# A gated linear attention with a maxout FFN: the carried state as a dense tile, its products with q per head, and a new order of all steps

## The chip, the cores and the metric

The kernel runs on one core of a Trainium2 chip. The metric is the device time of one execution in microseconds (us). All times here are of the same inputs, drawn once.

## The reference, cut to what matters

```python
# q, k, v, alpha: 4 x 8 x 768 x 48 (batch, heads, sequence, head size)
for t in range(S):
    state = alpha[:, :, t, :, None] * state + einsum('bhd,bhe->bhde', k[:, :, t], v[:, :, t])
    y[:, :, t] = einsum('bhd,bhde->bhe', q[:, :, t], state)
x = y.transpose(0, 2, 1, 3).reshape(3072, 384)
h = maximum(maximum(x @ w1, x @ w2), x @ w3)      # 384 -> 768
out = h @ w_out                                   # 768 -> 384
```

The first part is a recurrence over 768 positions with a state of 48 x 48 numbers for each of 32 heads; the second an ordinary matrix product with a maximum of three.

## The kernel before

**Tiling of the attention.** Each of the 12 windows `n` covers 256 positions of one batch (`c = n // 4` is the place in the sequence, `b = n % 4` the batch), all 8 heads. A position pair lies on one of 128 partitions (index `r` is which of the pair). The 128 partitions hold two sub-blocks `i` of 64 pairs, that is of 128 positions each. A window is worked in two units `u = 2n, 2n + 1` of four heads, counted in the texts as the even and the odd unit. Heads come in couples: `j` is the couple, `p` the head in it, and head `p` of a couple lies on partitions 64p to 64p + 47 once transposed.

**Steps of the attention.** `decay` squares alpha's pairs (`aa`), takes logarithms (`la`), and computes the factors by which the state decays (`hp`, `e`, `G`). `prep` sums the logarithms with a matmul (`Lp`, line 426), takes exponentials and scales q and k by them (`qk`, line 440) and v (`v`), then transposes q and k (`tp`, line 465) and evicts them (`qkT`, line 479). `attend` computes the scores of a unit as 16 small matmuls (`A`, line 491), and DVE masks and evicts them as `LA` (line 499). `state` sums k v over a sub-block (`pp`, line 523), and carries the state on: `grown` adds the decayed state to the sum (`add`, line 412, into `U` or `V`), `carry` decays it (`Z`, line 400). `output` multiplies q by the carried state (`yi`, line 556) and the scores by v (`ya`, line 578), both into the same PSUM bank, one bank for each sub-block; `xb` scales the result into SBUF, `xp` turns it (line 599), and `xT` holds the FFN's input.

**How the carried state is kept.** For each sub-block `i` and batch `b` there is a tile `Zs[i][b]` of 128 rows by 4 couples by 96 columns in 16 bits. Head 0 of a couple stands on rows 0 to 47 and columns 0 to 47, head 1 on rows 64 to 111 and columns 48 to 95; all else is zero from a memset at the start (line 228). So one matmul with 128 rows and 96 columns gives both heads' product with q. `carry` and `grown` write and read the two corners with an instruction each, on 48 rows.

**The FFN.** It is max(x w1, x w2, x w3) = x w1 + max(0, x (w2 - w1), x (w3 - w1)). `differences` makes the two differences (`d`, line 308) once the weights are there. `ffn` computes for each window 6 gate steps (`gp`, line 622, 6 matmuls of 256 columns each); ACT or DVE takes the positive part of the first of each couple (`h0`, lines 631 and 633), DVE the maximum with the second (`h1`, line 638). `op` then multiplies x by `past` = w1 w_out (line 655) and h by w_out (line 658) into one bank; `ob` evicts it and `out` stores it. `past` itself is computed once by `bypass` (`wt`, `w1T`, `mp`, line 334).

**The order.** Nothing is scheduled at run time. Each call of `plan.step` adds a step with its dependences, and `emit` walks through the string `ORDER`, one token for each step: its number, the letter of the engine that gets it (P for PE, V for DVE, A for ACT, G for POOL, S for SP), and the PSUM banks. Each engine then works its own steps strictly in that order. Loads and outputs are issued on SP, the four weight loads (`w1s`, two halves of `wcat`, `wo`) on POOL, between its other steps. There are 8 PSUM banks, shared by all.

## Time and profile before

| | us |
|---|---|
| median of 3 runs | 151.62 |
| lowest and highest | 150.16, 151.63 |
| the profiled execution, first to last instruction (its span) | 148.5 |
| lies around the span, by the lowest and the median run | 1.6 to 3.1 |
| PE busy | 130.6 (88% of the span) |
| DVE busy | 121.9 (82%) |
| ACT busy | 80.7 (54%) |
| POOL busy | 71.8 (48%) |

The profile is of an execution of its own, whose time outside the span isn't recorded; it is bounded by the runs. Busy time of PE is from modelled ends, and two small matmuls in different parts of the array count as one stretch. In the lists a row gives line, engine, operation, what it writes and reads, the shape, the count, then busy time and the mean in nanoseconds of one, then the idle time ahead of it and what ended that. PEld is the loading of the stationary operand.

### The profile page before, as it was taken

The numbers are of one execution on the slowest core, as the hardware profiler recorded it, in microseconds if no ns is written. First come the engines' busy times: TensorE is split into PE (matmuls) and PEld (weight loads), VectorE is DVE, ScalarE is ACT, GpSimd is POOL, SyncE is SP. The second block draws the span as 40 slices with busy tenths as digits, with TensorE's granted clock in tenths as the row PEclk, the third lists the DMA queues.
The fourth block names the chain that finished last, engine by engine and source line by source line (L and its number), as shares of the span: only waits on it lengthen the run. The fifth ranks groups of instructions, "written<-read, shape, count | busy, mean of one in ns | idle before, by whom it ended". The sixth has DMA issues, their size and how long they took to land.

```text
span 148.5 us, 5617 instructions
## 1 busy us (share of the span) xinstructions
PE 130.6 (88%) x2389; PEld 101.7 (68%) x2389; DVE 121.9 (82%) x231; ACT 80.7 (54%) x182; POOL 71.8 (48%) x114
## 2 busy tenths in 40 slices
PE   0136588889999999999999999999999999999990
PEld 0025576767776678887687889777777788787670
DVE  6489996999899979998896899699698786789720
ACT  3665156796895987947877759328622820000011
POOL 8105810431859888999976678994720100000000
PEclk9999999999999999999999999999999999999999
DMA  4999999999999999999997299601211100031223
GB/s 111 257 261 262 258 214 212 279 231 265 270 262 265 261 275 267 262 288 268 233 279 188 79 246 280 200 3 60 106 57 57 53 4 0 4 119 40 85 99 134
DMA packets 54728, 26.34 MB, mean 177 GB/s; under 512 B 50736, under 2 KB 54320, under 8 KB 54704
## 3 DMA queue, kind: packets, MB, share of 16 engines
q1 hardware_dynamic: 53584, 23.60, 63.4%
q0 software_dynamic: 832, 2.36, 8.1%
q8 instruction: 18, 0.29, 0.9%
q10 hardware_dynamic: 288, 0.04, 0.3%
q14 instruction: 6, 0.05, 0.1%
HBM read 23.63 MB, written 4.72 MB: 191 GB/s over the span
## 4 chain that ended last, share of the span: by engine, by line
PE 65%; DMA 10%; POOL 6%; ACT 5%; DVE 4%; SPq 4%; issue 3%; POOLq 0%; DVEq 0%
PE psum L622 26%; PE psum L658 15%; PE psum L655 8%; DMA wcat<-in_moe_w_dram 6%; SPq L274 4%; DMA qn<-in_q_dram 4%; POOL qk L440 3%; PE psum L491 3%; PE psum L578 3%; PE psum L465 2%; PE psum L599 2%; PE psum L334 2%; PE psum L556 2%; PE psum L523 2%; POOL Z L400 1%
## 5 line engine op out<-in xcount | busy, mean ns | idle before, releaser
L622 PE MATMUL psum<-xT,d 128*128 128x256 f16 x432 | 54.1, 273 | 0.9 <-DVE d L308 0.5
L622 PEld LDWEIGHTS <-d 128*128 128x128 f16 x432 | 40.0, 98 | 7.0 <-DVE d L308 1.5
L499 DVE TENSOR_TENSOR LA<-psum,d 128x1024 f16<-128x1024 f32 x24 | 28.7, 1218 | 3.7 <-PE psum L491 2.8
L658 PE MATMUL psum<-wo,hT 128*128 128x384 f16 (+1 forms) x150 | 27.5, 320 | 0.0
L638 DVE TENSOR_TENSOR hT<-psum,hT 128x512 f16<-128x512 f32 x36 | 23.7, 681 | 2.9 <-PE psum L622 2.6
L440 POOL TENSOR_TENSOR qk<-qn,ep 128x384 f16<-128x384 f32 x18 | 18.3, 1026 | 11.3 <-DMA qn<-in_q_dram 9.2
L631 ACT ACTIVATE hT<-psum 128x512 f16<-128x512 f32 x28 | 16.4, 601 | 12.7 <-PE psum L622 12.3
L255 ACT COPY ob<-psum 128x384 f32<-128x384 f32 x14 | 6.7, 481 | 27.8 <-PE psum L658 27.8
L658 PEld LDWEIGHTS <-hT 128*128 128x128 f16 x150 | 14.5, 98 | 8.9
L440 POOL TENSOR_TENSOR qk<-kn,en 128x384 f16<-128x384 f32 x16 | 15.9, 999 | 9.0 <-ACT en L435 8.5
L479 DVE COPY qkT<-psum 128x1024 f16<-128x1024 f16 x24 | 16.0, 683 | 0.9 <-PE psum L465 0.7
L655 PE MATMUL psum<-past,xT 128*128 128x384 f16 (+1 forms) x75 | 15.8, 320 | 0.0
L259 ACT ACTIVATE xb<-psum,c 128x384 f16<-128x384 f32 x17 | 9.3, 583 | 9.0 <-PE psum L578 9.0
L435 ACT ACTIVATE en<-psum 128x384 f32<-128x384 f32 x24 | 11.5, 493 | 2.1 <-DVE psum L430 2.1
L465 PE MATMUL psum<-d,qk 64*128 64x64 f16 x384 | 8.8, 198 | 4.1 <-POOL qk L440 2.1
L435 ACT ACTIVATE ep<-psum 128x384 f32<-128x384 f32 x24 | 11.6, 493 | 1.1 <-DVE psum L430 0.8
L351 POOL TENSOR_TENSOR aa<-an 128x384 f32<-128x384 f32 x9 | 9.0, 1001 | 4.7 <-DVE qkT L479 4.2
L255 ACT CAST xT<-psum 128x384 f16<-128x384 f32 x20 | 9.4, 482 | 3.0 <-PE psum L599 2.8
L426 PE MATMUL psum<-la,c 128*128 128x192 f16 x24 | 6.1, 271 | 5.5 <-ACT la L361 5.5
L465 PEld LDWEIGHTS <-qk 64*128 64x128 f16 x384 | 7.0, 99 | 5.5 <-DVE qk L440 2.9
L400 POOL TENSOR_TENSOR Z<-U,G 48x192 f16<-48x192 f32 x10 | 5.0, 504 | 11.8 <-DVE U L412 11.5
L430 DVE TENSOR_TENSOR psum<-psum,la 128x192 f32<-128x192 f32 x24 | 8.5, 358 | 2.6 <-PE psum L426 1.8
(58 smaller groups left out, 196.4 us busy)
## 6 DMA issues: line engine op xcount, KB each, us to landing
out_dram<-ob SPq DMA_DIRECT2D x23, 192.0 KB, 2.0
an<-in_alpha_dram SPq DMA_DIRECT2D x11, 384.0 KB, 6.2
qn<-in_q_dram SPq DMA_DIRECT2D x11, 384.0 KB, 5.7
kn<-in_k_dram SPq DMA_DIRECT2D x11, 384.0 KB, 6.2
vn<-in_v_dram SPq DMA_DIRECT2D x11, 384.0 KB, 6.3
wcat<-in_moe_w_dram POOLq DMA_DIRECT2D x2, 576.0 KB, 10.3
w1s<-in_moe_w_dram POOLq DMA_DIRECT2D x1, 576.0 KB, 7.9
wo<-in_moe_w_out_dram POOLq DMA_DIRECT2D x1, 576.0 KB, 7.8
```

Source lines behind the costliest of these rows:

```text
L255: (nc.scalar.copy if eng == "ACT" else nc.vector.tensor_copy)(out=out, in_=in_)
L259: nc.scalar.activation(out=out, in_=in_, func=AFT.Copy, scale=factor)
L435: lambda eng, t=t, sign=sign: nc.scalar.activation(out=t, in_=live[Lk], func=AFT.Exp, scale=sign),
L440: lambda eng, w=w, x=x, e=e: on[eng].tensor_mul(qk[:, w, :, :, :D].rearrange("p r h d -> p h r d"), ld[x][n % NL][:, hs], e),
L465: nc.tensor.transpose(live["tp", v][:, i, at:at + HALF], qks[v % NQ][rows, w, r, 2 * j:2 * j + 2, :], ident[rows, rows])
L479: lambda eng: nc.vector.tensor_copy(out=qkT.rearrange("p i w j t -> p i (w j t)"), in_=live["tp", u]),
L499: lambda eng: nc.vector.tensor_mul(LA.rearrange("p a j r t -> p (a j) (r t)"), live[Ak].rearrange("p a (j t) -> p (a j) t", j=2), maskA.un ...
L622: nc.tensor.matmul(live[gk][:, jj, :], hidden(apart[g][j][:, kt], jj), xT[:, kt, :], start=(kt == 0), stop=(kt == NFT - 1))
L631: nc.scalar.activation(out=h, in_=live[gk], func=AFT.Relu)
L638: lambda eng, h=h, gk=gk: nc.vector.tensor_max(h, live[gk], h),
L655: nc.tensor.matmul(live[ok], xT[:, kt, i * P:(i + 1) * P], past[:, kt, cols], start=(kt == 0), stop=False)
L658: nc.tensor.matmul(live[ok], hT[:, kt, i * P:(i + 1) * P], wo16[:, kt, cols], start=False, stop=(kt == NJ - 1))
```

## The change

`Zs` is now 128 rows by 4 couples by 48 columns: each head's state stands on its own rows, and the columns are shared, so the tile is dense (its padding rows hold what the sums give there). `carry` and `grown` are one instruction each over all 128 rows; the memsets of `Zs` are gone.

The product with q is taken per head: 48 rows of q and of the state, 48 columns, 8 matmuls for each sub-block in place of 4. They are split in two halves. The crossed ones, (sub-block 0, head 1) and (sub-block 1, head 0), are a step `yi` of their own for both sub-blocks together; the scores `A` of the odd unit wait for it. The others, (0, 0) and (1, 1), stand within `ya`, which now runs the odd unit's products with v first, then these, then the even unit's. `ya` therefore holds the two banks from `yi` on.

There are 777 steps where there were 821, and `ORDER` is new throughout: places, engines and banks of all steps. Read off the two strings: POOL has 36 `qk`, 16 `v`, 12 `aa` and 8 `Z` (34, 14, 9 and 23 before), DVE 12 `qk`, 1 `aa`, 12 `Z` of both kinds and 16 `add` (14, 4, 17 and 32), 12 `ob`, 9 `h0`, 2 `w1T` and 1 `past` (11, 8, 0 and 0). Ahead of the first gate step PE has the same attention steps of windows 0 and 1. Twelve gate steps of windows 0 and 1 then follow almost in a row, where the order before has ten among the attention of window 2. After the last attention output 12 gate steps are left (15 before). PE's last step is the second part of a half-wide `op` of the last 128 rows (a full-wide `op` before). The load of `w_out` is issued by POOL behind `aa` and `G0` of window 2.

```diff
@@ ORDER: the first and the last line of each @@
-0S 3S 53S 6S 7S 5S 2S 1S 11V 12A 8V 13A 4S 10A 28P0 9A 54S 14P1 29V 17P2 57V 55S 30A 18V 31A 56S
...
-818P 794P7 811A 816S 812S 819V 820S 795A 796S
+3S 11G 0S 1S 8G 9A 13A 26P0 10A 17P7 51S 56A 18V 19A 21G 55V 20A 12A 57A 61P7 27V 29A 71P1 72V 2S
...
+763P6 765P4 769P3 764V 770P 771V 772S 766P 767A 768S 773P6 774P 775A 776S
@@ -194,7 +191,7 @@
     obs = homes(4, [P, DM], FP32, "ob")
     U0s = homes(2, [P, NP, D], FP32, "U")
     U1s = homes(B, [P, NP, D], FP32, "V")
-    Zs = [homes(B, [P, NP, 2 * D], FP16, f"Z{i}_") for i in range(2)]
+    Zs = [homes(B, [P, NP, D], FP16, f"Z{i}_") for i in range(2)]
     e12s = homes(6, [P, NP, UB, 2], FP32, "e")
     G0s = homes(2, [P, NP], FP32, "G")
     G1s = homes(2, [P, NP], FP32, "H")
@@ -223,9 +220,6 @@
         nc.vector.memset(t[:, :, :, D:], 0.0)
     for t in qks:
         nc.vector.memset(t[:, :, :, :, D:], 0.0)
-    for eng, zz in ((nc.gpsimd, Zs[0]), (nc.vector, Zs[1])):
-        for t in zz:
-            eng.memset(t, 0.0)
 
     plan = Plan()
     place = {}
@@ -392,26 +386,17 @@
 
 
     def carry(engines, Zn, U, G, rank, reads, writes):
-        for p in range(2):
-            rows, cols = slice(p * DP, p * DP + D), slice(p * D, (p + 1) * D)
-
-            def run(eng, rows=rows, cols=cols):
-                src = live[U] if isinstance(U, tuple) else U
-                on[eng].tensor_mul(Zn[rows, :, cols], src[rows],
-                                   G[rows].unsqueeze(2).broadcast_to([D, NP, D]))
-
-            plan.step("Z" if "POOL" in engines else "Zp", engines, rank, run,
-                      reads=[U if isinstance(U, tuple) else (*reads[0], p), *reads[1:]],
-                      writes=[(*writes[0], p)])
+        def run(eng):
+            src = live[U] if isinstance(U, tuple) else U
+            on[eng].tensor_mul(Zn, src, G.unsqueeze(2).broadcast_to([P, NP, D]))
+
+        plan.step("Z" if "POOL" in engines else "Zp", engines, rank, run, reads=reads,
+                  writes=writes)
 
 
     def grown(U, key, Z, rank, Zk, to):
-        for p in range(2):
-            rows, cols = slice(p * DP, p * DP + D), slice(p * D, (p + 1) * D)
-            plan.step("add", "DVE", rank,
-                      lambda eng, rows=rows, cols=cols: nc.vector.tensor_add(
-                          U[rows], live[key][rows], Z[rows, :, cols]),
-                      reads=[key, Zk[p]], writes=[(*to, p)], size=0.6)
+        plan.step("add", "DVE", rank, lambda eng: nc.vector.tensor_add(U, live[key], Z),
+                  reads=[key, Zk], writes=[to], size=0.6)
 
 
     def prep(u):
@@ -470,15 +455,16 @@
                   reads=[("qk", v % NQ, w) for v in units for w in range(2)],
                   writes=[tk], size=len(units))
         for v in units:
-            attend(v, tk)
-
-
-    def attend(u, tk):
+            qkT = qkTs[v % NT_]
+            plan.step("qkT", "DVE", v,
+                      lambda eng, v=v, qkT=qkT: nc.vector.tensor_copy(
+                          out=qkT.rearrange("p i w j t -> p i (w j t)"), in_=live["tp", v]),
+                      reads=[tk], writes=[("qkT", v % NT_)])
+
+
+    def attend(u):
+        n, hh = divmod(u, 2)
         qkT, LA, Ak = qkTs[u % NT_], LAs[u % NT_], ("A", u)
-        plan.step("qkT", "DVE", u,
-                  lambda eng: nc.vector.tensor_copy(
-                      out=qkT.rearrange("p i w j t -> p i (w j t)"), in_=live["tp", u]),
-                  reads=[tk], writes=[("qkT", u % NT_)])
 
         def scores(eng):
             live[Ak] = banks2(Ak, FP32)
@@ -494,7 +480,7 @@
                                 qkT[rows, i, 0, j, :], start=True, stop=True)
 
         plan.step("A", "PE", u, scores, banks=[Ak],
-                  reads=[("qkT", u % NT_)], writes=[Ak])
+                  reads=[("qkT", u % NT_)] + [("crossed", n)] * hh, writes=[Ak])
         plan.step("LA", "DVE", u,
                   lambda eng: nc.vector.tensor_mul(
                       LA.rearrange("p a j r t -> p (a j) (r t)"),
@@ -527,7 +513,7 @@
 
         plan.step("pp", "PE", rank, sums, banks=keys, writes=keys,
                   reads=[("qk", u % NQ, 1) for u in us] + [("v16", u % NQ) for u in us])
-        Z0, Z1 = ([("Z", i, b, p) for p in range(2)] for i in range(2))
+        Z0, Z1 = ("Z", 0, b), ("Z", 1, b)
         if c == 0:
             carry("DVE", Zs[1][b], keys[0], G0s[n % 2], rank,
                   [keys[0], ("G0", n % 2)], [("Z", 1, b)])
@@ -540,34 +526,46 @@
             grown(U1s[b], keys[1], Zs[1][b], rank, Z1, ("V", b))
 
 
-    def output(n):
+    def carried(n):
         c, b = divmod(n, B)
         us = (2 * n, 2 * n + 1)
         keys = [("yp", n, i) for i in range(UB)]
         old = [c > 0 or i > 0 for i in range(UB)]
         rank = 2 * n + 1
 
-        def inter(i):
-            live[keys[i]] = bank(keys[i], [P, H, D], FP32)
+        def inter(pairs, first):
             for hh in range(2):
                 qkT = qkTs[us[hh] % NT_]
                 for j in range(2):
-                    h = 4 * hh + 2 * j
-                    nc.tensor.matmul(live[keys[i]][:, h:h + 2, :], qkT[:, i, 0, j, :],
-                                     Zs[i][b][:, 2 * hh + j, :], start=(h == 0), stop=False,
-                                     skip_group_check=True)
-
-        for i in range(UB):
-            if old[i]:
-                plan.step("yi", "PE", rank, lambda eng, i=i: inter(i), banks=[keys[i]],
-                          writes=[keys[i]],
-                          reads=[("Z", i, b, p) for p in range(2)]
-                          + [("qkT", u % NT_) for u in us])
+                    for i, p in pairs:
+                        if not old[i]:
+                            continue
+                        rows = slice(p * DP, p * DP + D)
+                        nc.tensor.matmul(live[keys[i]][:, 4 * hh + 2 * j + p, :],
+                                         qkT[rows, i, 0, j, :], Zs[i][b][rows, 2 * hh + j, :],
+                                         start=(first and hh == 0 and j == 0), stop=False,
+                                         skip_group_check=True)
+
+        def crossed(eng):
+            for i in range(UB):
+                if old[i]:
+                    live[keys[i]] = bank(keys[i], [P, H, D], FP32)
+            inter(((0, 1), (1, 0)), True)
+
+        plan.step("yi", "PE", rank, crossed, banks=[keys[i] for i in range(UB) if old[i]],
+                  writes=[keys[i] for i in range(UB) if old[i]] + [("crossed", n)],
+                  reads=[("Z", i, b) for i in range(UB) if old[i]] + [("qkT", u % NT_) for u in us])
+
+        return inter, keys, old, us, rank
+
+
+    def output(n, inter, keys, old, us, rank):
+        c, b = divmod(n, B)
 
         def intra(hh):
             LA, v16 = LAs[us[hh] % NT_], v16s[us[hh] % NQ]
             for i in range(UB):
-                if hh == 0 and not old[i]:
+                if hh and not old[i]:
                     live[keys[i]] = bank(keys[i], [P, H, D], FP32)
             for j in range(2):
                 for p in range(2):
@@ -577,13 +575,18 @@
                             h = 4 * hh + 2 * j + p
                             nc.tensor.matmul(live[keys[i]][:, h, :], LA[rows, p, j, r, :],
                                              v16[rows, 2 * j + p, r, :],
-                                             start=(h == 0 and r == 0 and not old[i]),
+                                             start=(h == HH and r == 0 and not old[i]),
                                              stop=(r == 1), skip_group_check=True)
 
-        plan.step("ya", "PE", rank, lambda eng: [intra(hh) for hh in range(2)],
+        def attended(eng):
+            intra(1)
+            inter(((0, 0), (1, 1)), False)
+            intra(0)
+
+        plan.step("ya", "PE", rank, attended,
                   banks=[keys[i] for i in range(UB) if not old[i]], writes=keys,
-                  reads=[("LA", u % NT_) for u in us]
-                  + [("v16", u % NQ) for u in us])
+                  reads=[("LA", u % NT_) for u in us] + [("v16", u % NQ) for u in us]
+                  + [("Z", i, b) for i in range(UB) if old[i]] + [("qkT", u % NT_) for u in us])
         for i in range(UB):
             m = 2 * n + i
             xb, yk, xk = xbs[m % 3], keys[i], ("xp", n, i)
@@ -689,7 +692,10 @@
                 for g in WAFTER.get(j, ()):
                     weights(g)
         state(n)
-        output(n)
+        shared = carried(n)
+        for u in (2 * n, 2 * n + 1):
+            attend(u)
+        output(n, *shared)
         if n == 3:
             differences()
             bypass()
```

81 lines of the change are left out of this document (39 added, 42 removed).

## The prediction

> **What bounds the kernel now.** I read the page's busy rows and slices first, then stretches cut at the times where the work changes, then the chain that ended last for the price of each step.
>
> ```profile
> PE 130.6 (88%) x2389; PEld 101.7 (68%) x2389; DVE 121.9 (82%) x231; ACT 80.7 (54%) x182; POOL 71.8 (48%) x114
> PE   0136588889999999999999999999999999999990
> DVE  6489996999899979998896899699698786789720
> PEclk9999999999999999999999999999999999999999
> ```
>
> ```profile
> 0.00:26.00 26.00, 13.00 (x306) 10.07 (x306) 20.62 (x48) 12.93 (x30) 9.69 (x24) 1.00 1.06 225
> 26.00:50.40 24.40, 23.07 (x431) 17.32 (x433) 23.00 (x46) 19.51 (x45) 13.86 (x19) 1.00 1.17 262
> 50.40:101.10 50.70, 50.42 (x1075) 40.66 (x1068) 44.79 (x84) 36.15 (x85) 42.90 (x65) 1.00 0.86 218
> 101.10:145.30 44.20, 44.08 (x593) 33.67 (x592) 33.46 (x57) 11.72 (x26) 5.33 (x9) 1.00 0.17 60
> ```
>
> The four stretches give PE, PEld, DVE, ACT and POOL busy time. Until 26 us PE is half idle and the DMA engines are full (share 1.06). From 26 to 101 PE is nearly always busy, and so is DVE: 23.0 of 24.4, then 44.8 of 50.7. After 101 it is PE alone, at a full clock. A busy PE is not a PE at its peak, though, so I price its steps where they run undisturbed:
>
> ```profile
> 89.90 0.51 PE psum L578 x32
> 90.40 0.47 PE psum L465 x32
> 94.09 0.57 PE psum L491 x32
> 94.66 0.24 PE psum L523 x16
> 98.45 0.49 PE psum L655 x3
> 98.94 0.97 PE psum L658 x6
> 99.91 0.17 PE psum L556 x4
> 100.66 0.40 PE psum L578 x32
> 130.49 4.58 PE psum L622 x42
> 145.22 0.48 ACT ob L255
> ```
>
> ```profile
> 5.49 0.32 PE L426 MATMUL psum<-la,c 128*128 128x192 f16 x1 [5.49 <-ACT la L361]
> ```
>
> The first fence is the chain (start, length, step), the second the timeline of PE, its first matmul. A gate product costs 109 ns (4.58/42), a step of six 0.66 us; a down projection 1.46 us; a small tile 12.5 to 18 ns; a carried product (L556) 42 ns. Times the counts (432, 207 full and 18 half-wide, 384 each of L465, L491 and L578, 320 of L523, 80 of L556, and some 11 us for the rest) this makes about 119 us. PE works from 5.49 to 145.2, 139.7 us, so some 21 us are lost. The 306 matmuls ahead of 26 us (64 in each of the four small-tile steps, 3.8 us, and 50 others, some 2.6) need about 6.4 of 20.5 us: 14 us are lost there, to loads and the first attention chain, and about 7 behind it. So in the middle and end time is PE work, with a small loss that DVE shares in; the end is 3.3 us of eviction and output behind the last matmul.
>
> **Part 1, the carried state.** Today each carry and each sum is two instructions on 48 rows; the change makes it one on 128.
>
> ```profile
> L430 DVE TENSOR_TENSOR psum<-psum,la 128x192 f32<-128x192 f32 x24 | 8.5, 358 | 2.6 <-PE psum L426 1.8
> L412 DVE TENSOR_TENSOR U<-psum,Z 48x192 f32<-48x192 f32 x16 | 5.7, 354 | 2.2 <-PE psum L523 1.9
> L412 DVE TENSOR_TENSOR V<-psum,Z 48x192 f32<-48x192 f32 x16 | 5.5, 351 | 0.3
> L400 POOL TENSOR_TENSOR Z<-V,H 48x192 f16<-48x192 f32 x13 | 6.8, 528 | 1.1 <-DVE H L388 0.6
> L400 POOL TENSOR_TENSOR Z<-U,G 48x192 f16<-48x192 f32 x10 | 5.0, 504 | 11.8 <-DVE U L412 11.5
> L440 POOL TENSOR_TENSOR qk<-qn,ep 128x384 f16<-128x384 f32 x18 | 18.3, 1026 | 11.3 <-DMA qn<-in_q_dram 9.2 <-ACT ep L435 2.0
> L261 DVE TENSOR_SCALAR xb<-psum,c 128x384 f16<-128x384 f32 x7 | 4.3, 611 | 0.2
> ```
>
> DVE takes 0.358 us for 128 rows of 192 (L430) and 0.354 for 48 (L412): rows are free, so the merged instruction keeps the price of one half. Sums: 32 to 16, 16 x 0.353 = 5.6 us less DVE. Carries: 40 to 20; read off the two orders, POOL's go from 23 to 8 (15 x 0.515 = 7.7 us less), DVE's from 17 to 12 (5 x 0.36 = 1.8 less). The memsets of Z go; they run before the first load lands, and are worth nothing. The new order also moves other work: DVE loses three squarings of alpha and two q/k products and gains two w1T copies and single evictions, which about cancel. POOL gains three squarings, two q/k and two v products, which eat most of what it saves (a q/k product is 1.03 there). Net: DVE about 7 us less, POOL and ACT 2 to 5 less.
>
> What is that worth? In 50.4 to 101.1 lie 6.98 us of L412 and 1.74 of DVE's L400:
>
> ```profile
> 50.40:101.10 50.70, 6.98 (x20) 1.00 0.86 218
> 50.40:101.10 50.70, 1.74 (x5) 9.20 (x19) 1.00 0.86 218
> ```
>
> Half, 4.4 us, leaves DVE there. It lies beside PE work; PE at the prices above would need about 48 of those 50.7 us. So the gain is between 0 (cover complete) and 2.7 (all of PE's loss was DVE's). I take 1.0, nearer the low end, since PE's busy row is 50.42 of 50.70. **-1.0.**
>
> **Part 2, the products.** 80 matmuls of 128 rows by 96 become 160 of 48 rows by 48, on the same kind of 64x128 tile as L578's. Those are the nearest row: 12.5 to 16 ns each, since neighbours lie in different halves of the array. 160 x 14 = 2.2 us against 80 x 42 = 3.4: **-1.1**. The change alternates halves too, but only where both sub-blocks have an old state; in the first four windows the four crossed ones all lie in one half. Bounds: at 12.5 ns -1.4; at the old 42 ns each, +3.3.
>
> The Trainium skill ("TensorE: Matmul & The Clock Gate", Back-to-back issue gap and the floors before it) says starts never come closer than about 25 ns however few columns. By that floor the products would cost 160 x 25 = 4.0 us, +0.6 where the sum has -1.1. The trace disagrees for alternating halves: 32 starts in 0.40 us.
>
> **Part 3, the head.** The order of the first eleven loads changes but they are the same ones. DVE now has k of window 1 (qk of unit 2) in front of qkT of unit 1.
>
> ```profile
> 8.10 1.42 SPq L274 DMA_DIRECT2D kn<-in_k_dram  x1
> ```
>
> ```profile
> 26.79 0.82 POOL L288 DMA_DIRECT2D wo<-in_moe_w_out_dram  x1
> ```
>
> ```profile
> 26.04 0.83 PE L622 MATMUL psum<-xT,d 128*128 128x256 f16 x6 [0.51 <-DVE d L308]
> ```
>
> ```profile
> kn<-in_k_dram SPq DMA_DIRECT2D x11, 384.0 KB, 6.2
> wo<-in_moe_w_out_dram POOLq DMA_DIRECT2D x1, 576.0 KB, 7.8
> ```
>
> ```profile
> L499 DVE TENSOR_TENSOR LA<-psum,d 128x1024 f16<-128x1024 f32 x24 | 28.7, 1218 | 3.7 <-PE psum L491 2.8 <-issue 0.7
> L638 DVE TENSOR_TENSOR hT<-psum,hT 128x512 f16<-128x512 f32 x36 | 23.7, 681 | 2.9 <-PE psum L622 2.6
> L479 DVE COPY qkT<-psum 128x1024 f16<-128x1024 f16 x24 | 16.0, 683 | 0.9 <-PE psum L465 0.7
> L308 DVE TENSOR_TENSOR d<-wcat,w1s 128x768 f16<-128x768 f16 x6 | 3.6, 618 | 1.2 <-DMA wcat<-in_moe_w_dram 1.2
> ```
>
> These are the issue of window 1's k on SP, of wo on POOL, PE's first gate product, the times from issue to landing, and DVE's groups. That k lands at about 8.1 + 6.2 = 14.3. Behind it on DVE stand the q/k product, three qkT (0.68), three LA (1.22), four carry steps (0.35), three xb (0.61) and one difference (0.62): about 10 us, so 24.3, and some 1 us of waits between engines. Transposing and one d make the first gate product start at 26 to 26.7 against 26.04, so the memsets and the earlier first weights buy nothing: **+0.3** (0 to 0.7).
>
> From there to 50 us the new order runs twelve gate steps almost in a row: 7.9 us of PE, while DVE has six differences (3.7), two w1T copies (1.2 by the d row) and six h1 (4.1), 9.0 us. DVE is 1 us late there, and wo, which POOL issues only behind G0 of window 2 (and that waits for ACT's e), goes out about 0.8 us later than 26.79 and lands 7.8 after that, just where the product w1 x w_out needs it. The old order loses about 3 us in the same stretch to the same causes. SP's queue holds the same 52 loads and 25 outputs, 36 loads ahead of the first output where it was 32; it gives and costs nothing. I take **0**, from -1.5 (the run is dense) to +2 (both lags land on the chain).
>
> **Part 4, the new wait.** Scores of the odd unit now wait for the crossed products, those for the second state, that for DVE's sum, that for L523. Unhurried: 0.35 + 0.36 to 0.5 + three hand-overs, about 1.2 us. The order sets other PE work between: in window 4 a score step, two gate steps and a turn, 0.28 + 0.66 + 0.66 + 0.17 = 1.8 us; in window 6 2.7. Queued behind the crossed step on PE are the scores, then gate steps, and behind these the evictions. With that cover: 0. The attended step now takes the odd unit's LA first, which is ready last; that removes 0.2 us of cover, which other steps replace.
>
> **Part 5, the tail.** The last PE step is now a half-wide one. Its eviction falls from 0.48 to about 0.3 and its output from 192 to 96 KB:
>
> ```profile
> out_dram<-ob SPq DMA_DIRECT2D x23, 192.0 KB, 2.0
> out_dram<-ob SPq DMA_DIRECT2D x2, 96.0 KB, 1.7
> L255 DVE COPY ob<-psum 128x192 f32<-128x192 f32 x2 | 0.7, 358 | 2.0 <-PE psum L658 1.9
> ```
>
> 0.2 + 0.3, less a little since two other outputs go out just before it: **-0.4** (-0.6 to +0.3).
>
> **Sum.** -1.0 - 1.1 + 0.3 + 0 + 0 - 0.4 = -2.2 on a span of 148.5, 146.3. The runs have 151.62 as median and 150.16 as lowest, so 1.6 to 3.1 us lie around the span; that stays. Predicted 149.4; its own range, from the bounds above, is 148.2 to 150.4.
>
> **Rivals.** (a) DVE's relief counts in full: 2.7 instead of 1.0, and the dense run at 26 us brings its 1.5, so 146.2 to 147.7, about 147.0. For it: DVE's 23.0 of 24.4. Against: PE's 50.42 of 50.70. Chance 0.15. (b) It is hidden: DVE's time lies beside PE's and only products and tail count, less the head and a little of DVE's lag (+0.6): -1.1 - 0.4 + 0.3 + 0.6 = -0.6, 151.0. The 25 ns case lands here too. Chance 0.22. (c) Slower: the crossed products arrive late. If DVE stands in an LA (1.22) when L523 ends, and POOL in a q/k product (1.0) when the sum is done, the chain is 1.22 + 0.35 + 1.0 + 0.5 + 0.3 = 3.4 against 1.8 to 2.7 of cover: about 1 us lost in each of windows 4 to 9, and PE in order stands still for it. -2.2 + 6 = +3.8: 155.4. For it: POOL is 42.9 of 50.7 busy in 50 to 101, and its Z today waits 11.5 us for U without harm only because nothing in front of the scores needs it. Against: in most windows the order puts sum and carry of the state on DVE directly ahead of LA. It decides once the windows lose over 0.4 us each. Chance 0.30. That the merged carry costs more than one half (the change doing less than it says) is ruled out by L430 against L412.
>
> **Numbers.** Forecast 0.33, (a) 0.15, (b) 0.22, (c) 0.30. A measurement of this kernel tells about 1% from no change, 150.1 to 153.1. Faster: forecast and (a), 0.48; same: (b), 0.22; slower: 0.30. The range for 8 in 10 takes in (a) down to 146.6 and most of (c) up to 155.0.
>
> **What would show it.** Right: L412 and L400 with 16 and 20 instructions at unchanged means; L578's stretch with 8 more matmuls at under 16 ns; first gate product near 26 us; PE waiting under 0.3 us per window at the crossed products; 3 us behind the last matmul. Wrong: idle time of PE in front of the crossed line released by Z, or of DVE's LA by L491; a first gate product past 27.5; carried products at over 25 ns.

## The result, and the profile after

The changed kernel takes 155.55 us (median of 4, 154.55 to 155.88) where the kernel before, on the same chip, takes 150.89 (150.15 to 151.63). The ratio is 1.0306, with an interval of 1.0247 to 1.0365: 3% slower, where 149.4 and faster was forecast. The profiled execution took 155.88 us, of which 154.2 are its span; before, the span was 148.5. Most kernels below that load alpha of window 1 earlier have executions on two levels, near 151 and near 156; a ratio is of the lower level unless the text says otherwise, and the executions are listed where the level is the question.

The page of the changed kernel, busy rows and slices, and its stretches (PE, PEld, DVE, ACT and POOL busy time), cut 4.4 us later than those of before since the work behind the first cut starts that much later:

```profile
PE 131.8 (85%) x2469; PEld 100.6 (65%) x2469; DVE 118.8 (77%) x206; ACT 76.8 (50%) x175; POOL 68.9 (45%) x102
PE   0126168999997998999999989999999999999991
DVE  4058997768988888999997797999977695767630
```

```profile
0.00:30.40 30.40, 13.66 (x320) 10.80 (x321) 20.17 (x38) 12.39 (x29) 12.46 (x25) 1.00 1.04 233
30.40:54.80 24.40, 23.19 (x382) 16.55 (x382) 20.64 (x36) 16.14 (x38) 15.93 (x21) 1.00 1.18 259
54.80:105.50 50.70, 49.45 (x1093) 38.58 (x1091) 45.57 (x82) 35.51 (x84) 36.77 (x50) 1.00 0.76 187
105.50:151.10 45.60, 45.49 (x678) 34.66 (x678) 32.37 (x52) 12.46 (x25) 3.74 (x6) 1.00 0.20 64
```

PE does the same work ahead of the first gate product, in 30.4 us where it was 26.0. In the third stretch it is busy 49.45 of 50.70 (50.42 before). From the first gate product to PE's end it is 120.7 us (30.43 to 151.10) against 119.2, and 3.1 lie behind it against 3.3. So of 5.7 us more span 4.4 are the head, 1.5 the rest, and the tail gives 0.2 back.

The timeline at the place where the head is lost, after, DVE then POOL then PE (start, length):

```profile
13.88 1.23 DVE L485 TENSOR_TENSOR LA<-psum,d 128x1024 f16<-128x1024 f32 x1 [0.40 <-PE psum L477]
15.03 2.94 DVE L425 TENSOR_TENSOR qk<-kn,en 128x384 f16<-128x384 f32 x1
17.89 0.68 DVE L460 COPY qkT<-psum 128x1024 f16<-128x1024 f16 x1
...
14.83 1.00 POOL L425 TENSOR_TENSOR qk<-qn,ep 128x384 f16<-128x384 f32 x1
15.78 0.99 POOL L425 TENSOR_TENSOR qk<-kn,en 128x384 f16<-128x384 f32 x1
16.72 0.60 POOL L285 DMA_DIRECT2D wcat<-in_moe_w_dram  x1
17.34 0.21 POOL L377 TENSOR_TENSOR G<-e 128x4 f32<-128x4 f32 x1
17.50 1.32 POOL L425 TENSOR_TENSOR qk<-qn,ep 128x384 f16<-128x384 f32 x1
...
18.89 0.23 PE L544 MATMUL psum<-Z,qkT 48*128 48x48 f16 x2 [3.84 <-DVE Z L391]
...
30.43 0.82 PE L625 MATMUL psum<-xT,d 128*128 128x256 f16 x6
```

and the same DVE product in the kernel before, with a copy of `qkT` ahead of it:

```profile
11.63 0.69 DVE L479 COPY qkT<-psum 128x1024 f16<-128x1024 f16 x1
...
14.81 1.44 DVE L440 TENSOR_TENSOR qk<-kn,en 128x384 f16<-128x384 f32 x1
```

DVE's k product of unit 2 reads two operands from SBUF. Undisturbed it takes 0.55 us; here it takes 2.94, while POOL runs products with two SBUF operands of its own. Behind it stand `qkT` of unit 1 (17.89; that copy went at 11.63 before), the carry, the sum, and the crossed step on PE, which waits 3.84 us for `Z`. The Trainium skill ("SBUF — State Buffer", Who interferes with whom) says that DVE with two SBUF inputs contends with a GpSimd instruction that reads SBUF, since the second input comes through a shared interface. These rows agree: 2.94 against 0.55.

The groups of the merged instructions and of the products they share engines with, after (busy, mean ns), and DVE's k products before:

```profile
L398 DVE TENSOR_TENSOR V<-psum,Z 128x192 f32<-128x192 f32 x8 | 2.8, 354 | 0.6
L398 DVE TENSOR_TENSOR U<-psum,Z 128x192 f32<-128x192 f32 x8 | 2.7, 353 | 2.2 <-ACT ob L249 1.1 <-PE psum L509 0.8 <-POOL qk L425 0.3
L391 POOL TENSOR_TENSOR Z<-V,H 128x192 f16<-128x192 f32 x4 | 2.0, 507 | 4.3 <-DVE H L382 4.3
L391 DVE TENSOR_TENSOR Z<-U,G 128x192 f16<-128x192 f32 x4 | 2.7, 666 | 0.3
L425 DVE TENSOR_TENSOR qk<-kn,en 128x384 f16<-128x384 f32 x7 | 8.0, 1153 | 0.0
```

```profile
L440 DVE TENSOR_TENSOR qk<-kn,en 128x384 f16<-128x384 f32 x8 | 5.2, 659 | 0.0
```

Sums and carries are as forecast, 0.35 on DVE and 0.51 on POOL for all 128 rows, half as many. But the `Z` with both operands in SBUF costs DVE 0.67, and the k products 1.15 on average instead of 0.66.

### The profile page after: what moved, and what is told of

It reads as the page before. It is cut to its first block, busy times and chain, and to the rows that moved or that the text cites. A ratio compares the mean times of both kernels' runs of the same rounds, so it can differ in the third digit from the quotient of the medians.

```text
span 154.2 us, 5750 instructions
## 1 busy us (share of the span) xinstructions
PE 131.8 (85%) x2469; PEld 100.6 (65%) x2469; DVE 118.8 (77%) x206; ACT 76.8 (50%) x175; POOL 68.9 (45%) x102
## 4 chain that ended last, share of the span: by engine, by line
PE 64%; issue 11%; DVE 9%; DMA 9%; ACT 3%; SPq 1%; POOL 1%; DVEq 0%; ACTq 0%; POOLq 0%
PE psum L625 24%; PE psum L661 14%; PE psum L658 8%; DMA wo<-in_moe_w_out_dram 5%; PE psum L477 4%; DMA an<-in_alpha_dram 3%; PE psum L450 3%; PE psum L576 3%; DVE qk L425 3%; PE psum L602 2%; PE psum L544 2%; DVE qkT L460 2%; PE psum L509 2%; PE psum L328 1%; PE psum L411 1%
## 5 line engine op out<-in xcount | busy, mean ns | idle before, releaser
L625 PE MATMUL psum<-xT,d 128*128 128x256 f16 x432 | 53.5, 273 | 0.4 <-DVE LA L485 0.4
L661 PE MATMUL psum<-wo,hT 128*128 128x384 f16 (+1 forms) x150 | 27.5, 320 | 0.0
L425 POOL TENSOR_TENSOR qk<-qn,ep 128x384 f16<-128x384 f32 x19 | 19.9, 1056 | 8.6 <-ACT ep L420 8.6
L634 ACT ACTIVATE hT<-psum 128x512 f16<-128x512 f32 x27 | 15.7, 604 | 16.0 <-PE psum L625 12.4
L425 POOL TENSOR_TENSOR qk<-kn,en 128x384 f16<-128x384 f32 x17 | 17.0, 1006 | 4.1 <-ACT en L420 3.0
L411 PE MATMUL psum<-la,c 128*128 128x192 f16 x24 | 5.3, 266 | 9.2 <-ACT la L355 9.0
L255 POOL TENSOR_SCALAR v<-vn,c 128x384 f16<-128x384 f32 x16 | 10.3, 648 | 5.2 <-DMA vn<-in_v_dram 5.2
L477 PE MATMUL psum<-qkT 48*64 48x128 f16 x384 | 10.9, 236 | 1.6 <-DVE qkT L460 0.8
L450 PE MATMUL psum<-d,qk 64*128 64x64 f16 x384 | 9.5, 198 | 2.6 <-DVE qk L425 2.1
L249 ACT COPY ob<-psum 128x384 f32<-128x384 f32 (+1 forms) x13 | 6.1, 469 | 11.0 <-PE psum L661 7.9
L345 POOL TENSOR_TENSOR aa<-an 128x384 f32<-128x384 f32 (+1 forms) x12 | 11.1, 933 | 0.8 <-DMA an<-in_alpha_dram 0.8
```

The costliest lines, as they stand in the source:

```text
L249: (nc.scalar.copy if eng == "ACT" else nc.vector.tensor_copy)(out=out, in_=in_)
L425: lambda eng, w=w, x=x, e=e: on[eng].tensor_mul(qk[:, w, :, :, :D].rearrange("p r h d -> p h r d"), ld[x][n % NL][:, hs], e),
L450: nc.tensor.transpose(live["tp", v][:, i, at:at + HALF], qks[v % NQ][rows, w, r, 2 * j:2 * j + 2, :], ident[rows, rows])
L477: nc.tensor.matmul(live[Ak][i * HALF:(i + 1) * HALF, p, at:at + P], qkT[rows, i, 1, j, r * HALF:(r + 1) * HALF], qkT[rows, i, 0, j, :], st ...
L625: nc.tensor.matmul(live[gk][:, jj, :], hidden(apart[g][j][:, kt], jj), xT[:, kt, :], start=(kt == 0), stop=(kt == NFT - 1))
L634: nc.scalar.activation(out=h, in_=live[gk], func=AFT.Relu)
```

## Experiments

**Which half of the change is it?** The first kernel has the carried state and the products of before, in the new order; the other two have the new form in the order of before.

```diff
 old_form_new_order: ORDER of the change; a merged Z/add token becomes two, one for each 48 rows;
                     yi per sub-block, all of it at the place of the new crossed step
 new_form_old_order: ORDER of before; a pair of Z/add tokens becomes one at the second's place;
                     the odd unit's A moves behind the crossed step
 ..._late_ya:        that, and ya one to three PE steps later in seven windows
```

> The state stays block-diagonal (two instructions for each carry and sum, products of 128 rows by 96 columns, no crossed step), but every step stands where the new order puts it. Theory 'the order is slow': about as slow as the changed kernel, 154 to 157 us, with the first gate product near 30 us. Rival 'the new form is slow' (crossed products in front of the odd scores, more changes of tile size): 149 to 152 us.

> The new form (dense state, products per head, crossed half ahead of the odd scores) in the old order: each merged step stands where its second half stood, the odd unit's scores and their eviction are moved behind the crossed products, all else keeps its place and engine, but for 6 banks. Since the old form in the new order took 168.3 us against 155.5, the theory 'the form helps, the order loses' expects no more than the 150.0 of the kernel before, 147 to 150 us, first gate product at 26 to 27 us. Rival 'both lose, the old form merely fits the new order badly': over 151.5 us.

> As the one before, with at least 0.9 us of other PE work between the odd scores and the attended step, so that the eviction of the scores has time. If the odd scores' late place costs (PE standing in front of the attended step), this is 0.5 to 2 us faster than the one before; if not, the same within 0.5 us.

Measured: 168.33 us for the old form in the new order (ratio 1.1194, 1.1097 to 1.1291), 166.83 for the new form in the old order (1.1087, 1.1051 to 1.1124), 172.41 with the later `ya` (1.1468, 1.1408 to 1.1528). So neither half stands alone, and the theory that the form helps and the order loses fell. The new order was set for the merged instructions: with the old form in it DVE is busy 133.5 us in place of 118.8. The old order was set for another list of steps than the new form has. Two of the waits of PE in the new form in the old order:

```profile
PE psum L576 <- DVE LA L485: 4.1, 5, 1.4
PE psum L450 <- DVE LA L485: 3.9, 3, 1.4
```

Here PE stands for the copies `LA` of the scores; at the crossed step itself it stands only 0.4 us. My reading was that the odd scores, now behind the crossed step, come late. The kernel with the later `ya` was to show it, and does not: it was expected 0.5 to 2 us faster or the same, and is 5.6 us slower. Why these two lose 16 us and more stays open. But the timeline of the old form in the new order shows the head's stall again, to the hundredth of a microsecond:

```profile
15.20 2.94 DVE L439 TENSOR_TENSOR qk<-kn,en 128x384 f16<-128x384 f32 x1
```

So the stall belongs to the order and not to the state's form.

**What makes the head late?** Three edits of the order near its start, alone and together.

```diff
 weights_first (POOL)
-w1s, qk(u2 q), qk(u3 k), wcat, G0, qk(u3 q), wcat
+w1s, wcat, wcat, qk(u2 q), qk(u3 k), G0, qk(u3 q)
 alpha_third (SP; on ACT la of window 1 behind unit 1's instead of ahead of the first exponentials)
-alpha, alpha, q(window 0), alpha(window 1), k ...
+alpha, alpha, alpha(window 1), q(window 0), k ...
 head_mended = both, and on DVE
-LA(0), qk(u2 k), qkT(1), Z, add
+LA(0), qkT(1), Z, add, qk(u2 k)
```

> The changed kernel, with POOL issuing both halves of wcat right behind w1s, ahead of its three q/k products of window 1. Theory 'DVE's q/k product at 15.03 us takes 2.94 us since POOL's products hold it up': with POOL at its issues just then it falls under 1.2 us, the first gate product comes 1 to 2 us earlier than 30.4, the time falls by 1 to 2 us. Rival 'it waits for data from a load': length and time stay within 0.3 us.

> The changed kernel, with window 1's alpha as the third load in place of the fourth, and ACT taking its logarithm behind the first exponentials. Theory 'ACT stands behind a late load and the whole first chain with it': the first exponential moves from 8.2 to about 6.4 us, the transposed q/k of unit 0 from 12.2 to under 11, and the time falls by 1 to 2 us if nothing further on catches it. Rival 'the later wait on DVE for window 1's k catches it': first exponential earlier, first gate product within 0.5 us of 30.4, time the same.

> Both edits above together, and DVE's q/k product of unit 2 moved behind the transposed q/k, carry and sum of unit 1 and window 0. Theory 'the loss is made ahead of the first gate product': it comes near 26.5 us, and the time is 151.0 to 152.5 us. Rival 'the order loses it further on anyway' (PE later stands at loads, DVE or w_out): first gate product near 26.5, time still over 153.5 us.

Measured: 152.96 (1.0157, 1.0068 to 1.0247), 152.99 (1.0147, 1.0052 to 1.0242), 153.29 with a spread of 151.39 to 156.52 (1.0148, 1.0042 to 1.0254). By the ratios each edit alone takes back some 2.3 us, and together they give no more. In the first DVE's k product takes 0.79, since POOL's products start behind the weights' issues, and the first gate product comes at 28.01, 2.42 earlier than 30.43. Of this 2.15 are the stall (2.94 less 0.79); the rest is that DVE came to the product 0.35 earlier (14.68 for 15.03). Alpha is still late there.

In alpha_third the first exponential moves from 8.2 to 6.4 us and `qkT` of unit 0 from 12.2 to 10.3, as expected. DVE and POOL then, in its profiled execution (154.64, of the upper level):

```profile
14.18 0.56 DVE L425 TENSOR_TENSOR qk<-kn,en 128x384 f16<-128x384 f32 x1 [0.99 <-DMA kn<-in_k_dram]
...
14.23 1.37 POOL L425 TENSOR_TENSOR qk<-kn,en 128x384 f16<-128x384 f32 x1 [0.29 <-DMA kn<-in_k_dram]
```

DVE is early enough to wait for k, starts 0.05 us ahead of POOL's second product, and is not held. So the two losses are not independent: alpha's late place also made DVE late enough to meet POOL's products. What this execution loses comes behind that: alpha of window 2 takes 11.9 us to land, and the first gate product stands at 29.42. In the profile of head_mended, its slowest execution, the moved product is held again (3.0 us), and alpha of window 2 lands late too (13.8 us), as below.

> The changed kernel, with DVE's q/k product of unit 2 given to POOL, behind POOL's first one; the weight loads come out later by one product (1 us), not earlier. Theory 'the two engines' products hold each other up': unit 1's transposed q/k is evicted near 15.2 us instead of 17.9, the first gate product comes 1 to 2 us earlier than 30.4 although the weights are later, time 153 to 154.5. Rival 'what helped in the run with weights first was the earlier weights': first gate product no earlier than 30, time 155 or more.

This one gives unit 2's k product to POOL too, with loads and weights as in the change. 159.22 (1.0483, 1.0391 to 1.0575): slower than the change itself. The first gate product came earlier than expected (27.61), but then the weights' difference on DVE, which reads two SBUF operands too, met POOL's next stream:

```profile
28.80 8.06 DVE L302 TENSOR_TENSOR d<-wcat,w1s 128x768 f16<-128x768 f16 x3 [0.58 <-DMA wcat<-in_moe_w_dram]
...
L302 DVE TENSOR_TENSOR d<-wcat,w1s x6: 552/570/5722, 26.3 to 35.0; 128x768 f16<-128x768 f16 x6
```

One of the six took 5.72 us (least, median, longest in the second row): it ended at 35.0, and POOL worked without a break from 29.7 to past that. I had not expected that: taking one collision away made a longer one.

**Both edits, and the kernel before with one.**

> The changed kernel with both edits that each brought its ratio from 1.031 to 1.015: weights first on POOL, and alpha of window 1 third with its logarithm behind the first exponentials. If the two losses of the head are separate (a late load, and DVE held up by POOL) they add: 149 to 151 us, first gate product at 26 to 27 us. If one hides behind the other: 152 to 153.5.

> The kernel before the change, with the same move of both halves of wcat behind w1s on POOL. There one q/k product on DVE at 14.8 us takes 1.44 us for 0.55. If products on both engines hold each other up and the weights set the first gate product, it falls to under 0.7 and the first gate product comes 0.5 to 1.5 us before 26.0: 0.3 to 1% faster than before. If PE catches up by itself: the same.

The first has executions at 155.72, 157.38, 151.77 and 156.43, so that neither expectation holds. In the profiled one (155.72) DVE's k product starts at 14.05, 0.10 us behind POOL's first (13.95), and takes 3.38. The kernel before with its weights first: 150.54, ratio 1.0007 (0.9970 to 1.0044). Its product took 0.92 instead of 1.44, where under 0.7 was expected, and nothing was gained: there `qkT` of unit 1 doesn't stand behind it, and POOL's k product, for which PE's transposes wait, moved from 14.83 to 15.95. The first gate product came at 26.74, later than the 26.04 of before.

**Taking the collision away.** Of unit 2, DVE forms the q product, whose load lands 1.5 us earlier, and POOL the k product: in the change's own order, and with both edits.

```diff
-DVE: qk(u2 k)    POOL: qk(u2 q)
+DVE: qk(u2 q)    POOL: qk(u2 k)
```

> The changed kernel as it is, loads and weights as in the change, and only the two products of unit 2 exchanged between DVE and POOL (DVE q, POOL k). Theory (the hold-up of DVE's k product is the larger part of the loss): the first gate product comes 1.5 to 3 us before 30.4, at 27.5 to 29, and the time is 152 to 153.5. Rival (alpha as fourth load alone sets the head, and the held product lies in its shadow): the first gate product stays after 29.5 and the time at 154.5 or more.

> The kernel with the weights first and alpha third, and one thing more: of unit 2, DVE forms the q product, whose load lands at about 12.6 us, and POOL the k product, whose load lands at about 14; until now it was the other way round, and DVE's k product met POOL's stream of products. Theory (what is left of the loss is DVE's k product of window 1 held up by POOL): the q product takes 0.6 to 1.2 us, qkT of unit 1 ends before 15, the first gate product stands at 26 to 27.5, and the time is 149 to 151 in every execution, with no second group at 155 to 157. Rival (the new order as a whole costs PE time behind the head, by its crossed steps): the head is mended as said, but the time stays at 151.5 to 153. Second rival (the collision only moves to the next DVE product): a DVE step with two inputs in SBUF takes over 2 us somewhere before 30 us, and the time stays at 155 or more.

Alone: 155.41 (1.0326, 1.0274 to 1.0379). In the profiled execution, its quickest (154.03), the first gate product comes at 28.97, as the theory had it, but the median did not fall. The exchange alone doesn't take the collision away: DVE reaches its product at 14.33, 0.2 behind POOL's first, and it takes 2.17. With both edits one execution took 150.26 and five 155.50 to 158.48. The quick one, profiled:

```profile
13.12 0.55 DVE L425 TENSOR_TENSOR qk<-qn,ep 128x384 f16<-128x384 f32 x1
13.59 0.68 DVE L460 COPY qkT<-psum 128x1024 f16<-128x1024 f16 x1
...
14.04 1.95 POOL L425 TENSOR_TENSOR qk<-kn,en 128x384 f16<-128x384 f32 x2
...
26.28 7.37 PE L625 MATMUL psum<-xT,d 128*128 128x256 f16 x66
```

The product runs its 0.55 ahead of POOL's, and the head is that of before (26.28 against 26.04). DVE's first `xb` shows how much each cause takes: the first gate product follows 6.2 us behind it in all these kernels where alpha of window 2 is in time. In the change, weights_first, alpha_third and q_for_k:

```profile
24.23 0.62 DVE L255 TENSOR_SCALAR xb<-psum,c 128x384 f16<-128x384 f32 x1
21.82 0.62 DVE L255 TENSOR_SCALAR xb<-psum,c 128x384 f16<-128x384 f32 x1
21.00 0.62 DVE L255 TENSOR_SCALAR xb<-psum,c 128x384 f16<-128x384 f32 x1
20.08 0.62 DVE L255 TENSOR_SCALAR xb<-psum,c 128x384 f16<-128x384 f32 x1
```

From the change to weights_first 2.4 us go, with the stall and the 0.35 by which DVE was earlier (alpha of window 1 landed in 5.0 us there, 5.4 in the change). From there to alpha_third, where k is not held either, 0.8 go with alpha's place. The last 0.9 go where DVE no longer waits for k, which lands at 14.2, but forms the q product, whose load lands earlier. So 26.3 + 0.9 + 0.8 + 2.4 = 30.4, the 30.43 of the change, by one execution of each kernel. But what were the five others of q_for_k?

> As q_for_k, and DVE's q product of unit 2 stands ahead of the attended copy LA of window 0, so that DVE waits idle for its load (about 12.6 us) and takes it over a microsecond before POOL's products can start (their load lands at about 14). Theory (a late DVE meets POOL's stream, and this decides between the two levels of q_for_k): the product takes 0.6 us, LA of window 0 and all behind it comes 0.3 to 0.8 us later than in q_for_k's quick execution, the first gate product at 24.5 to 26, and all executions lie at 150 to 151.5, level with the kernel before. Rival (the two levels come from elsewhere, for instance from a later DVE product): executions at 155 and over remain.

> As q_first_in_queue, and LA of window 0 moves behind the carry and the sum of the first state, so that qkT of unit 1, on which the second window hangs, is not put off by it. Theory: qkT of unit 1 ends at about 14, as in q_for_k, LA of window 0 at about 16; the first gate product at 24 to 25.5; all executions at 149.5 to 151, level with the kernel before or up to 1% ahead. Rival (A of window 1 waits for the copy of A of window 0 out of its bank, and the gain is given back there): the first gate product at 26 or later and 151 to 152.5.

Here DVE takes the q product ahead of `LA` of window 0 and waits idle for its load (the second also sets that `LA` behind the sum). By the theory that a late DVE is the only cause the upper level had to go. It stayed, as the rival had it: five of 13 executions at 156.10 to 158.76, four of 12 at 156.41 to 158.01 (ratios 1.0082, 1.0031 to 1.0133, and 1.0046, 1.0007 to 1.0086). In the second's profiled execution (150.48) the first gate product stands at 26.61, not at the 24 to 25.5 expected. Of the first an execution of the upper level was profiled (158.76): SP's issues, POOL, PE.

```profile
11.21 1.25 SPq L268 DMA_DIRECT2D an<-in_alpha_dram  x1
12.51 1.37 SPq L268 DMA_DIRECT2D qn<-in_q_dram  x1
13.92 10.20 SPq L268 DMA_DIRECT2D kn<-in_k_dram  x1
...
12.15 0.74 POOL L285 DMA_DIRECT2D w1s<-in_moe_w_dram  x1
...
27.49 0.99 POOL L345 TENSOR_TENSOR aa<-an 128x384 f32<-128x384 f32 x1 [10.21 <-DMA an<-in_alpha_dram]
...
29.09 0.32 PE L411 MATMUL psum<-la,c 128*128 128x192 f16 x1 [7.15 <-ACT la L355]
```

No DVE product is held. Alpha of window 2, issued at 11.21, lands at 27.4, and PE stands 7.15 us at that window's `Lp`, with the first gate product behind it (33.56). The weights, issued at 12.15, came in between.

> As q_and_copy_first, and POOL scales v of unit 0 (0.58 us, until now ACT's) ahead of its three issues of expert weights, so that these go out at about 12.7 us instead of 12.15. Theory (in the runs with the weights first the second level comes from alpha of window 2: where SP has finished issuing it 0.3 us or more after the first weights' issue began, it lands 12 to 16 us later, behind the weights, instead of 6): alpha's issue ends at 12.3 to 12.6, before the weights', it lands at 17 to 18 in every execution, the first gate product comes at 26.5 to 27.5, and no execution lies at 155 or over; all at 150.5 to 152. Rival (the second level comes from something else): executions at 156 to 158 remain, three or four in ten.

```diff
-ACT: v(u0)       POOL: w1s, wcat, wcat
+                 POOL: v(u0), w1s, wcat, wcat
```

151.63, ratio 1.0045 (0.9998 to 1.0093), and 12 executions from 150.12 to 153.48, wider than the 150.5 to 152 expected: the upper level is gone.

```profile
11.21 1.25 SPq L268 DMA_DIRECT2D an<-in_alpha_dram  x1
...
12.79 0.74 POOL L285 DMA_DIRECT2D w1s<-in_moe_w_dram  x1
...
17.63 0.99 POOL L345 TENSOR_TENSOR aa<-an 128x384 f32<-128x384 f32 x1
...
26.90 7.52 PE L625 MATMUL psum<-xT,d 128*128 128x256 f16 x66
```

With the weights 0.64 us later alpha lands 5.6 us after its issue. So there were two causes of late heads. The stall is the changed kernel's own (its alpha of window 2 lands in 5.9 us). The late alpha of window 2 came in with my mending, which issues the weights at 12.1 us where the change does at 14.05. The five others of q_for_k can be either; none has a profile.

**What do the crossed products cost?** Three kernels leave out the crossed half, 80 matmuls, and so part of the output: on weights_and_alpha, q_for_k and value_before_weights.

> As weights_and_alpha, with the crossed half of the products with the carried state left out (80 of the 160 matmuls; the odd scores then wait for nothing). From the trace a crossed step costs about 0.3 us with its two changes of tile size, 12 of them 3.6 us, if PE is the bound: 2.5 to 4 us faster than weights_and_alpha. By the forecast's 14 ns each it would be 1.1 us faster. If the wait for the state in front of the odd scores costs 1 us a window besides, 8 us or more.

> The kernel before this one in the list, and the crossed half of the carried products is left out: 80 matmuls less, and part of the output is not computed. By the prediction's price (14 ns each) it is 1.1 us faster than that kernel, or nothing where other work hides them. By the trace's price (eight at 13 ns, 0.1 us until the scores join on behind them and 0.1 us ahead of them, in twelve windows) it is 2.5 to 4 us faster. Rival (waits for the second state's sum also count): more than 4 us.

> As value_before_weights, and the crossed half of the carried products is left out: 80 matmuls less, part of the output is not computed. By the prediction's 14 ns each it is 1.1 us faster than that kernel; by the trace's price (0.2 us for a crossed step of eight and 0.1 us ahead of it, in twelve windows, and half of that where only one sub-block has an old state) 2 to 3.5 us, where nothing else bounds; if DVE or the loads bound the windows, under 0.5 us.

The first two lie on two levels (150.66 to 157.67, ratio 1.0043, 0.9969 to 1.0116; 148.73 to 157.80, ratio 0.9997, 0.9961 to 1.0033) and tell little. The third is clean: 151.23, ratio 1.0049 (1.0011 to 1.0088) beside 1.0045 (0.9998 to 1.0093) with the products. PE's page row with them, then its products and row without:

```profile
PE 131.8 (89%) x2469; PEld 100.8 (68%) x2469; DVE 114.5 (77%) x206; ACT 76.4 (51%) x174; POOL 68.9 (46%) x103
```

```profile
L544 PE MATMUL psum<-Z,qkT 48*128 48x48 f16 x80 | 3.2, 183 | 0.0
PE 131.0 (88%) x2389; PEld 99.7 (67%) x2389; DVE 112.7 (76%) x206; ACT 76.5 (51%) x174; POOL 68.7 (46%) x103
```

PE saves 0.8 us and the time doesn't move: my expected 2 to 3.5 us were wrong, and "under 0.5" where something else bounds fits, though the two intervals leave about 0.6 us to either side. The time is 0.5% above the kernel before in both.

> As weights_and_alpha, with the output on which SP stands for some 11 us near 66 us moved behind five of the loads that wait behind it. Theory 'the stand costs nothing': within 0.5 us of weights_and_alpha, DMA's gap gone. Rival 'late loads starve windows 9 to 11': 1 us or more faster.

SP stands on one output from 66.5 to 77.9 us in the change, and no load is issued meanwhile. A version of the change with that output behind all seven loads that wait gave no time. Behind five, on weights_and_alpha: 156.60 (1.0396, 1.0312 to 1.0479, all four on the upper level, 155.38 to 157.62), a profile with both a held product (3.22) and alpha late (13.7 us). The three upper executions of weights_and_alpha lie at 155.72 to 157.38, so the rival's 1 us is not seen. With the head lost in two ways in it, that is weak evidence, and the output's share stays open.

No version of the change with its whole output was faster than the kernel before; the nearest, value_before_weights, is level with it.

## Why the prediction was wrong, step by step

**What bounds** was read rightly: behind the head PE is busy 118.1 of 120.7 us (117.6 of 119.2 before), and the mended kernels show how little is to be had there.

**Part 1.** Counts and prices of the merged instructions came out. "DVE about 7 us less" did not: DVE's busy time fell by 3.1. Most of the rest is the collision: 7 k products at 1.153 are 4.2 over 0.55 each, where 8 at 0.659 were 0.9. The step that failed is that every DVE duration was a row's mean, as if DVE and POOL were independent. The trace of before held the sign, a 1.44 us product at 14.81 beside POOL's at 14.83, and a group mean of 659 beside one of 553 for the same shape; I quoted neither. Of the gain of 1.0 at most 0.6 is seen, and only once the head is mended: value_before_weights takes 118.6 from first gate product to PE's end, 0.6 less than before, for Parts 1 and 2 together and by one execution of each. In the change itself that stretch is 1.5 longer, where the two parts together made it 2.1 shorter. A DVE product at 47.1 (1.35 us) keeps PE's transposes waiting 0.86 there. A carry at 58.1 takes 0.84, and PE stands 0.66 in the scores at 60.0, until 0.14 after the end of DVE's next `LA`; the trace names no releaser for that, so this second link is not shown.

**Part 2.** The chain of one window, after:

```profile
69.70 0.20 PE psum L544 x8
72.41 0.30 PE psum L576 x16
72.81 0.20 PE psum L576 x16
```

Eight straight products fit between the two `ya` rows (72.71 to 72.81): 12.5 ns each, as forecast, and half of the 25 that the prediction set beside it. The crossed step takes 0.20 for eight, and PE starts it 0.20 us after the start of a gate product, like its other steps on small tiles, where the steps on full tiles, the old products among them, start after 0.11. So 0.30 to 0.40 stand against two steps of 0.17: by these prices the term is about 0, not -1.1. What I left out is the change of tile shape at both ends of a step of its own. It made no difference to the end that the runs could tell: without the crossed products the time was the same.

**Part 3**, the head, is the step that failed most: +0.3 was +4.4. That is 4.1 of the 7.9 us by which the span misses the forecast (5.7 more in place of 2.2 less); 3.6 are the stretch behind the head, and 0.2 the tail. The sign of being wrong that came was a first gate product past 27.5. "That k lands at about 14.3" was right (it landed at 14.2, and DVE came to it at 15.03). "Behind it on DVE stand the q/k product, three qkT ..." left about 0.55 for that product (the other items make 9.55 of its 10 us), and it was 2.94. And "the order of the first eleven loads changes but they are the same ones" cost alpha of window 1's new place nothing: it stands ahead of k, its logarithm stands ahead of the first exponential on ACT (8.2 us, 6.2 before), and that is 0.8 by itself and what made DVE late for the product. The rest is the chain from k's landing, which was too short: with nothing held and alpha early, k's product starts at 14.18 and `xb` at 21.00, and with 6.2 behind that the first gate product would be near 27.2 (an estimate, since alpha_third loses more behind it), not 26 to 26.7. All three lie on the one chain the prediction had, which is why none was covered. The 24.4 us behind the first gate product came out as forecast: PE is busy 23.19 of them, against 23.07.

**Part 4** held. PE waits at the crossed line once, in the head, for what the stall delayed:

```profile
PE psum L544 <- DVE Z L391: 3.8, 1, 3.8
```

In windows 4 to 9 PE doesn't wait at that line. So rival (c) named 155.4 and the right side, and its mechanism was not the one: the figure is a coincidence. With the head mended rival (b), no difference, is what is left.

**Part 5**: 3.3 to 3.1 behind PE's end, half of the -0.4.

The forecast's own range ended at 150.4, with 0.7 at most for the head, a bound that came from undisturbed rows. The range for 8 in 10 reached 155.0 only by rival (c)'s waits in the windows, so it came near 155.55 for a reason that was not there.

## What to carry to other kernels

Before a DVE step with two SBUF operands is priced, look at what POOL runs at that time: if POOL has a stream of such steps, the price runs up to the length of that stream, and a tenth of a microsecond decides: 0.56 us for the product that started 0.05 ahead of POOL's (alpha_third), 3.38 for one 0.10 behind (weights_and_alpha). Moving instructions and loads near the start has to be priced along the chain to the first big product, with the engines' neighbours and the other queue's transfers, not by counts. And where an edit mends one collision, list what moves into the next one before trusting a mean of a few executions.

## What the runs showed of the hardware

DVE steps with two SBUF operands waited through several POOL instructions in a row, not one: 2.94 and 3.38 us for 0.55, 5.72 for 0.55. Where DVE reached its product first (13.12 against POOL's 14.04) it took 0.55.

A load on SP's queue came late where weights were issued on POOL's queue at about the same time. In nine kernels the weights went out at about 12.1. Where SP had finished issuing alpha of window 2 by 0.09 to 0.30 us after that moment (four kernels), it landed in 5.9 to 6.0 us; where by 0.31 to 0.49 (five), in 11.9 to 16.2. The queues of q_first_in_queue (packets, MB; the first is SP's loads and the outputs, the second the weights):

```profile
q1 hardware_dynamic: 53584, 23.60, 59.6%
q0 software_dynamic: 832, 2.36, 7.6%
```

A packet of the weights is 2.8 KB, one of the loads 0.44. The Trainium skill ("DMA: Bandwidth & Descriptors", Queues, rings and completion order) says that a DMA engine takes the queues in turn, a packet at a time; by that, as an estimate from these mean packets, the loads would get about a seventh of the bytes while weights run. In q_first_in_queue alpha landed at 27.4, behind the last weights (26.9). In alpha_third it landed at 23.2, with the first half of `wcat` (23.1) and ahead of the second (27.3). So it was not always the last weights that it waited for, and no run tries this mechanism. What the runs show is that with the weights issued 0.64 us later none of 12 executions lies on the upper level, and that alpha landed in 5.6 us in the one profiled. Why the border is so sharp stays open.
